# Streaming attention: five 4 MB buffers against 8 MB loads of 64 KB runs into a hand-kept ring of five slots

## The chip, the cores and the metric

The kernel runs on one core of one Trainium2 chip. The metric is the device time in microseconds (us) of one execution; most executions of one kernel agree within 0.3%. PE is the engine for matmuls, DVE the vector engine, ACT the scalar engine, POOL the engine for cross-partition work, SP the engine whose queue issues nearly all loads here. A profile is one execution; its span is some 2 us shorter than the time (1347.8 against 1349.4 us for the kernel before), and spans are compared with spans.

## The reference

One decoding step: attention of 4 queries (one for each batch element) with 32 heads over a K and a V cache of 8192 rows, plus a small gated feed-forward block. Cut to what matters, and partly put in words:

```python
def reference(A_x, A_k_cache, A_v_cache, A_wq, A_wo, B_x, B_w_r, B_w_gate, B_w_up, B_w_down, gate_w):
    # A_x 4x1x1024; k_cache, v_cache 4x32x8192x128; wq 1024x4096; wo 4096x1024; all bf16
    q = (x @ wq) split into 32 heads of 128
    scores = einsum("bhqd,bhkd->bhqk", q, k_cache) * Dh ** -0.5
    a = einsum("bhqk,bhkd->bhqd", softmax(scores), v_cache) -> (4, 1, 4096) @ wo
    b = x + upd     # upd: (silu(x @ w_gate) * (x @ w_up)) @ w_down, times sigmoid(x @ w_r)
    ...             # A_x, B_x and gate_w are combined at the end (cut)
```

K and V together are 537 MB, the weights 39 MB. Each byte is used once, so the kernel is a stream of loads with a little work on each.

## The kernel before

Each load is a 4 MB piece: two heads, each on 64 partitions, 128 rows of 128 numbers in each partition (32 KB per partition). Pieces go into a pool of five buffers. A K piece is transposed on DVE in four steps and multiplied on PE after each step; a V piece takes 32 matmuls with 512 columns. A group of K pieces ends with a softmax, which passes through POOL, DVE and ACT. V follows K by one group.

```python
    ring = ctx.enter_context(tc.tile_pool(name="ring", bufs=5))
    ...
    def slot():
        return ring.tile([P, RING], BF, name="piece", tag="piece")    # RING = 128*128: 32 KB per partition
    ...
    def kv_view(cache, u):
        b, h0 = heads(u)
        return cache[b, h0:h0 + HT].rearrange("h (r j) d -> (h r) (j d)", j=JR)      # HT = 2, JR = 128

    def k_piece(u):
        ...
        kn = slot()
        nc.sync.dma_start(out=kn[:], in_=kv_view(A_k_cache, u))
        for c in range(JR // CJ):                                                    # four steps
            T = ttp.tile([P, CJ, 2, 32, 2], BF, name="T", tag="T")
            nc.vector.transpose(...)                                                 # L336
            ...                                                                      # 8 matmuls into S_ps, L342
        if t == GT - 1:
            softmax(g)
    ...
    for u in range(NT - 2):
        order += [("k", u)] + [("v", u - LAG)] * (u >= LAG)
```

Only PE keeps the written order; on every other engine, and on the SP queue, a scheduler decides the order of instructions when the kernel is built. Each queue is then worked through in that order.

## Time and profile before

Three runs took 1349.28 to 1349.53 us, median 1349.34.

| what | before |
|---|---|
| time, span | 1349.3 us, 1347.8 us |
| bytes of the load queue | 575.68 MB |
| share of the span in which the load queue's packets were under way | 99.5% |
| PE, DVE busy | 79%, 47% |
| a 4 MB load, from issue to landing | 39.4 us |

The page of the profile, its rows of 40 slices (tenths of DMA busy), its queues, its chain of work that ended last, two groups of instructions and the loads of K (count, KB each, median us from issue to landing):

```profile
DMA  9999999999999999999999999999999999999997
DMA packets 22162, 576.22 MB, mean 428 GB/s; under 512 B 2399, under 2 KB 2407, under 8 KB 2925
q1 hardware_dynamic: 22104, 575.68, 99.5%
DMA 50%; PE 30%; DVE 11%; issue 6%; ACT 1%; POOL 1%; SPq 0%; DVEq 0%; ACTq 0%
L336 DVE STREAM_TRANSPOSE T<-piece 128x2048 uint32<-128x2048 uint32 x256 | 576.1, 2288 | 437.0 <-DMA piece<-in_A_k_cache_dram 321.1
L401 PE MATMUL o_ps<-piece,PB 128*16 128x512 bf16 x2048 | 457.6, 382 | 14.8 <-DMA piece<-in_A_v_cache_dram 14.8
piece<-in_A_k_cache_dram SPq DMA_DIRECT2D x64, 4096.0 KB, 39.4
```

(T is the transposed K; S_ps and o_ps are the sums of the K and of the V matmuls.) The stream of loads is the limit: it has no hole, and DVE's largest wait is for K (321.1 us). The chain names PE and DVE for 41% of the span all the same. That is no contradiction: the chain steps from a load to what let it be issued, which is a buffer coming free. As several loads lie queued, that release comes long before the stream needs it. 39.4 us from issue to landing, against 9.7 us that 4 MB take at the full rate, says that about four loads are queued at any time.

The waits of the SP queue before (us in total, times, longest) show the same: SP waits nearly all the time, and it costs nothing.

```profile
SPq L394 <- DVE T L336: 551.3, 57, 21.0
SPq L333 <- PE o_ps L401: 442.1, 52, 10.4
```

### The profile page before, as it was taken

How to read it: one execution, taken by the hardware profiler on the slowest of the kernel's cores; microseconds unless marked ns; L12 is line 12 of the kernel's file. 1: busy time of each engine (PE TensorE's matmuls, PEld its weight loads, DVE VectorE, ACT ScalarE, POOL GpSimd, SP SyncE). 2: the span in 40 equal slices, each digit the busy share in tenths (PEclk: the TensorE clock that was granted, in tenths of full speed). 3: DMA queues.
4: the chain of work that ended last, by engine and by line, in shares of the span. 5: the costliest groups of instructions: out<-in, count | busy, mean ns of one | idle time of the engine just before them, and what ended most of it. 6: DMA issues, size and time to landing. Idle time of an engine off the chain costs nothing.

```text
span 1347.8 us, 8253 instructions
## 1 busy us (share of the span) xinstructions
PE 1059.3 (79%) x4600; PEld 233.2 (17%) x2412; DVE 631.4 (47%) x375; ACT 41.5 (3%) x46; POOL 47.9 (4%) x115
## 2 busy tenths in 40 slices
PE   2667779876978868876998769888788859797878
PEld 0111111211111111111212111211112112121111
DVE  3555755535544554454545454444544456346000
ACT  0000010001000010001000010000000010000000
POOL 2000000000000000000000000000000000000000
PEclk8878989898989989989898879899888979999899
DMA  9999999999999999999999999999999999999997
GB/s 403 433 433 422 433 430 430 432 433 430 430 433 430 430 431 434 429 431 432 433 428 432 433 430 430 433 431 429 432 434 429 428 433 434 429 428 434 432 423 323
DMA packets 22162, 576.22 MB, mean 428 GB/s; under 512 B 2399, under 2 KB 2407, under 8 KB 2925
## 3 DMA queue, kind: packets, MB, share of 16 engines
q1 hardware_dynamic: 22104, 575.68, 99.5%
q8 instruction: 27, 0.44, 0.1%
q14 instruction: 11, 0.08, 0.0%
q10 hardware_dynamic: 20, 0.02, 0.0%
HBM read 575.68 MB, written 0.01 MB: 427 GB/s over the span
## 4 chain that ended last, share of the span: by engine, by line
DMA 50%; PE 30%; DVE 11%; issue 6%; ACT 1%; POOL 1%; SPq 0%; DVEq 0%; ACTq 0%
DMA piece<-in_A_k_cache_dram 40%; PE o_ps L401 16%; PE S_ps L342 13%; DVE T L336 10%; DMA piece<-in_A_v_cache_dram 9%; PE small L419 1%; DMA piece<-in_A_wo_dram 1%; POOL PB L373 1%; DVE PT L367 1%; ACT PTs L365 1%; ACT OS L411 1%; DVE OS L412 1%; POOL tot L377 0%; PE acc L188 0%; PE o_ps L225 0%
## 5 line engine op out<-in xcount | busy, mean ns | idle before, releaser
L336 DVE STREAM_TRANSPOSE T<-piece 128x2048 uint32<-128x2048 uint32 x256 | 576.1, 2288 | 437.0 <-DMA piece<-in_A_k_cache_dram 321.1
L342 PE MATMUL S_ps<-T,Z 128*128 128x512 bf16 x2048 | 544.6, 416 | 246.6 <-DVE T L336 235.3
L401 PE MATMUL o_ps<-piece,PB 128*16 128x512 bf16 x2048 | 457.6, 382 | 14.8 <-DMA piece<-in_A_v_cache_dram 14.8
L342 PEld LDWEIGHTS <-Z 128*128 128x128 bf16 x1024 | 108.0, 105 | 667.2 <-issue 664.3
L401 PEld LDWEIGHTS <-PB 128*16 128x16 bf16 x1024 | 91.9, 90 | 373.1 <-issue 361.3
L412 DVE SCALAR_TENSOR_TENSOR OS<-o_ps,mE,OS 128x512 f32<-128x512 f32 x16 | 12.0, 751 | 174.6 <-ACT OS L411 174.6
L326 POOL TENSOR_TENSOR Z<-qa,mq 128x16 bf16<-128x16 bf16 x64 | 16.7, 262 | 1072.3 <-PE S_ps L342 1054.3
L411 ACT ACTIVATE OS<-o_ps,mE 128x512 f32<-128x512 f32 x16 | 11.0, 687 | 1040.5 <-PE o_ps L401 1040.5
L419 PEld LDWEIGHTS small<-selg,OS 128*128 128x128 f32 x128 | 24.9, 273 | 12.2 <-issue 11.1
L419 PE MATMUL small<-selg,OS 128*128 128x8 f32 x128 | 22.3, 302 | 0.0
L353 DVE TENSOR_REDUCE m<-S_ps 128x1 f32<-128x1024 f32 x8 | 9.8, 1225 | 15.9 <-PE S_ps L342 15.9
L188 PE MATMUL acc<-piece,LT 128*4 128x512 bf16 x64 | 14.9, 378 | 1.7 <-DMA piece<-in_A_wo_dram 1.6
L373 POOL COPY PB<-PT 64x1024 bf16<-64x1024 bf16 x8 | 15.1, 1884 | 29.1 <-DVE rex L375 29.1
L372 ACT COPY PB<-PT 64x1024 bf16<-64x1024 bf16 x8 | 15.3, 1908 | 10.6 <-DVE PT L367 10.6
L367 DVE STREAM_TRANSPOSE PT<-PTs 128x1024 bf16<-128x1024 bf16 x8 | 10.0, 1245 | 11.9 <-ACT PTs L365 11.9
L188 PE MATMUL acc<-piece,hT 128*4 128x512 bf16 x56 | 12.4, 379 | 0.0
L131 PE MATMUL small<-identb,x 6*128 6x6 bf16 x8 | 0.6, 194 | 14.2 <-DVE identb L128 14.2
L379 DVE RECIPROCAL rinv<-tot 128x16 f32<-128x16 f32 x8 | 2.0, 253 | 19.9 <-POOL tot L377 19.9
L365 ACT ACTIVATE PTs<-S_ps,negm 128x1024 bf16<-128x1024 f32 x8 | 8.9, 1113 | 70.0 <-DVE negm L362 70.0
L225 PE MATMUL S_ps<-piece,xw 128*4 128x512 bf16 x64 | 6.6, 591 | 3.0 <-DMA piece<-in_A_wq_dram 3.0
L422 DVE SCALAR_TENSOR_TENSOR OT<-small,sgb,rinv 128x8 bf16<-128x8 f32 x16 | 3.2, 202 | 11.7 <-PE small L419 11.7
L358 POOL PARTITION_ALL_REDUCE gmx<-mex x8 | 3.1, 390 | 81.9 <-issue 50.3
(72 smaller groups left out, 74.6 us busy)
## 6 DMA issues: line engine op xcount, KB each, us to landing
piece<-in_A_k_cache_dram SPq DMA_DIRECT2D x64, 4096.0 KB, 39.4
piece<-in_A_v_cache_dram SPq DMA_DIRECT2D x63, 4096.0 KB, 39.1
piece<-in_A_wq_dram SPq DMA_DIRECT2D x2, 4096.0 KB, 22.1
piece<-in_B_w_gate_dram SPq DMA_DIRECT2D x2, 3584.0 KB, 40.1
piece<-in_B_w_up_dram SPq DMA_DIRECT2D x2, 3584.0 KB, 34.6
piece<-in_A_wo_dram SPq DMA_DIRECT2D x6, 1024.0 KB
piece<-in_B_w_down_dram SPq DMA_DIRECT2D x1, 4096.0 KB, 35.6
piece<-in_A_v_cache_dram SPq DMA_DIRECT2D x4, 1024.0 KB, 32.6
```

Of the source, the lines that this page charges most:

```text
L188: nc.tensor.matmul(out_ap, lhsT=lhsT, rhs=rhs, start=start, stop=True, skip_group_check=True)
L326: nc.gpsimd.tensor_tensor(out=Z[:, :, 31:31 + P].rearrange("p e (s d c) -> p e s d c", s=HT, d=QH)[:, :, :, :, 0], in0=qa[:, :, h0:h0 + HT ...
L336: nc.vector.transpose(out=T[:].rearrange("p j h i e -> p (j h i e)").bitcast(U32), in_=kn[:, c * CJ * Dh:(c + 1) * CJ * Dh].bitcast(U32))
L342: nc.tensor.matmul(sps[:, z, :], lhsT=Z[:, he, s:s + P], rhs=T[:, 16 * z:16 * z + 16, half, :, e], start=(t == 0 and c == 0 and he == 0), ...
L365: nc.scalar.activation(out=PTs[:], in_=sps[:].rearrange("p z n -> p (z n)"), func=ACT.Exp, bias=negm[:, 0:1], scale=scale, accum_out=rs[:, ...
L367: nc.vector.transpose(out=PT[:].rearrange("p j i -> p (j i)"), in_=PTs[:])
L372: nc.scalar.copy(out=Bv[0:W, :, :, 0, :], in_=Pv[0:W])
L373: nc.gpsimd.tensor_copy(out=Bv[W:P, :, :, 1, :], in_=Pv[W:P])
L401: nc.tensor.matmul(o_ps[row:row + NM, e, :], lhsT=B_[:, JT * t + c, z, w].rearrange("p e s j -> p (e s j)"), rhs=vn[:, j0 * Dh:(j0 + 4) * ...
L411: nc.scalar.activation(out=o_sb[:], in_=o_ps[:, 0, :], func=ACT.Copy, scale=mE[:, 0:1])
L412: nc.vector.scalar_tensor_tensor(out=o_sb[:], in0=o_ps[:, 1, :], scalar=mE[:, 1:2], in1=o_sb[:], op0=ALU.mult, op1=ALU.add)
L419: nc.tensor.matmul(oT[:, :], lhsT=o_sb[:, q * Dh:(q + 1) * Dh], rhs=selg[:, q].rearrange("p t s -> p (t s)"), start=(q == 0), stop=(q == 3))
```

## The change

Its intent: half as many packets, each twice as long. A load now brings 8 MB: four heads, each on a quadrant of 32 partitions, 64 KB in one run from the cache to each partition. It fills two neighbouring slots of a ring of five, kept by hand as one tile. The pairs take slots (0,1), (2,3), (4,0), (1,2), (3,4), and again; one pair in five wraps, and its destination is written with a step of −4 slots. The weights are loaded the same way, except wo and the last V pair, which come in smaller pieces. A K pair has eight transposes, a V pair 64 matmuls of twice as many output rows; the total work on DVE and PE is the same. A group of the softmax is now four pairs of four heads (it was eight pieces of two heads).

```diff
-    ring = ctx.enter_context(tc.tile_pool(name="ring", bufs=5))
+    NS = 5
+    ring = const.tile([P, NS, RING], BF, name="ring")
+    turn = [0]
+
+    def slots(n):
+        at = turn[0]
+        turn[0] = (at + n) % NS
+        return at
+
+    def load_pair(src, n):
+        a = slots(2)
+        step = 1 if a + 1 < NS else 1 - NS
+        dst = ring[:, a:a + 2, 0:n] if step == 1 else ring[:, NS - 1::1 - NS, 0:n]
+        ins = nc.sync.dma_start(out=dst, in_=src.rearrange("p (s n) -> p s n", s=2))
+        if n < RING:
+            WIDE[ins.ins.name] = 2 * n          # weights: the read is rewritten as one run (cut)
+        return [ring[:, a], ring[:, (a + 1) % NS]]
-        return cache[b, h0:h0 + HT].rearrange("h (r j) d -> (h r) (j d)", j=JR)
+        return cache[b, h0:h0 + NQ].rearrange("h (r j) d -> (h r) (j d)", j=2 * JR)
-        kn = slot()
-        nc.sync.dma_start(out=kn[:], in_=kv_view(A_k_cache, u))
-        for c in range(JR // CJ):
+        ks = load_pair(kv_view(A_k_cache, d), RING)
+        for n in range(RD):
+            kn, c = ks[n // JT], n % JT
-        vn = slot()
+            vs = load_pair(vv, RING)
     ... (masks, weights and softmax copies for four heads instead of two are cut)
```

## The prediction

> **What bounds the kernel now.** The DMA stream. The page's 40 slices show DMA at 9 tenths throughout and 422 to 434 GB/s; windows of 50 us show a DMA share of 1.00 and 426 to 433 GB/s. 575.7 MB at 431.5 GB/s is 1334 of the span's 1347.8 us; the rest is start and tail. PE is busy 79%, DVE 47%, and neither sets the pace: the largest DVE wait is for K transfers (321 us). The 4 MB transfers take 39 us from issue to landing, four times the 9.7 us that each needs: four lie queued, so the queue hides slow releases.
>
> **What the change brings.** Twice as long reads halve the packets (22,104 now). The Trainium skill (DMA: Bandwidth & Descriptors, "Where 436 GB/s comes from") puts the fabric's ceiling at 435 GB/s; the trace's 431.5 leaves at most 0.8%, 11 us. I expect about half: 5 us. Compute is the same: 256 transposes of 2.27 us, 2048 + 2048 matmuls of 512 columns.
>
> **What it costs.** Five slots hold two and a half 8 MB transfers of 19.4 us. Transfer n+1 needs slots of n-1 freed while n flies; that alone would fit: half a K pair is four transposes (8.9 us), half a V pair 32 matmuls (7.07 us), both under 19.4. But the built program's waits are wider for the transfers that wrap (slots 4 and 0, two in ten). They wait for the last transpose of the newest K pair, in slots they don't touch. And the scheduler then puts the next K load ahead of a wrapped V or weight load on the in-order SP queue. The same page says (Anatomy of one DMA) that waits are done on the issuing sequencer, so everything behind waits too. Walking the built order with the trace's durations (estimates; about 3 us from issue to landing beyond the transfer, as the first K piece shows: 12.6 MB issued from 0.8 us are there at 33.1):
> - Seven times (K1, K4, K9, K14, K19, K24, K29) a K load waits for half of the K pair just landed, with nothing in flight: 8.9 to 10 us of transposes + 3 = 12 to 13 us idle; 90 in all, and 10 more where the softmax of a group end delays DVE.
> - Seven times (up, V0, V5, V10, V15, V20, V25) the load after a wrapped one waits for that one to land and for half of its matmuls: 7 to 8.7 us + 3 = 10 to 12; 77 in all.
> - Six wrapped K loads wait for all eight transposes of the K pair before (18 us against a flight of 19.4): 2.6 each, 16 in all.
>
> DMA is the critical path, so all of it shows: 1349 + 193 - 5, less some 12 for a shorter start-up latency than I took: **1525 us**, range 1490 to 1560. Faster by 2%: 0.02; within 2%: 0.05; slower: 0.93.
>
> **What would show it.** Slices of the page with DMA at 4 to 7 tenths, about every 200 us, and 429 to 435 GB/s between; packets near 12,000; mean some 380 GB/s. In the SP queue's waits: loads waiting for transposes and o_ps matmuls in the order above, K1 before the gate's weights. In the chain: the K transfers' share down, transposes and o_ps up. Landing of K about 20 to 35 us for 8 MB. PEclk lower around the holes.
>
> **What would make it wrong.** If both sides of the wait are shorter than I think (idle restart under 3 us, PE warm), 1490. If 64 KB reads are slower per byte, later still. If the wide waits do not hold SP in the order built, the stream stays full and the time is about 1343 us.

## More of the kernel before

The third, fourth and fifth run are read for large differences only.

## The result, and the profile after

Four runs of the changed kernel took 1564.91 to 1566.71 us, median 1565.66, beside 1349.42 us for the kernel before on the same chip. The ratio is 1.1603, with a 95% interval of 1.1586 to 1.1619: 16% slower. (Ratios here are the mean time of one kernel's fast runs over that of the other's of the same rounds, so not quite the ratio of the medians.)

The same lines of the page after; the last but one is from the trace's full list of loads, and has no size as it takes in the K pairs of more than one form:

```profile
DMA  9689769995978996889996798996798976799997
DMA packets 13279, 576.20 MB, mean 368 GB/s; under 512 B 1326, under 2 KB 1334, under 8 KB 1852
q1 hardware_dynamic: 13224, 575.68, 86.2%
DMA 52%; PE 23%; issue 14%; DVE 10%; POOL 1%; ACT 1%; DVEq 0%; SPq 0%; ACTq 0%
L356 DVE STREAM_TRANSPOSE T<-ring 128x2048 uint32<-128x2048 uint32 x256 | 570.2, 2281 | 663.3 <-DMA ring<-in_A_k_cache_dram 370.3
L428 PE MATMUL o_ps<-ring,PB 128*32 128x512 bf16 x2048 | 463.6, 388 | 164.7 <-DMA ring<-in_A_v_cache_dram 164.7
ring<-in_A_k_cache_dram SPq DMA_DIRECT2D x26, 28.7
ring<-in_A_k_cache_dram SPq DMA_DIRECT2D x6, 8192.0 KB, 22.7
```

The work per instruction is unchanged: 256 transposes at 2281 ns instead of 2288, 2048 V matmuls at 388 ns instead of 382. What changed is the first row: the stream has holes, and the load queue is under way for 86.2% of a longer span. Multiplied by the spans, the shares give a simple ledger: 0.862 × 1565.0 = 1349 us of transfer instead of 0.995 × 1347.8 = 1341, so 8 us more; and 216 us idle instead of 7, so 209 us more. (The shares are rounded; the packet times themselves add up to 1348.3 and 1340.9 us, so 7.4 us more.) The spans differ by 217 us. Six K loads, the wrapped ones, now land 22.7 us after they were issued (the median); 8 MB alone take 19.4 us, so nothing was in front of them: they were issued into an empty queue.

The waits of the SP queue after:

```profile
SPq L128 <- DVE T L356: 536.4, 45, 21.0
SPq L128 <- DMA ring<-in_A_k_cache_dram: 408.6, 24, 41.0
SPq L128 <- DMA ring<-in_A_v_cache_dram: 216.0, 12, 32.8
SPq L128 <- PE o_ps L428: 211.9, 24, 10.8
```

The total of waits on transposes is hardly changed (it was 551 us). What is new are the long waits for landings, 408.6 and 216.0 us, where the K and V loads of the kernel before waited 23.7 us for landings of K and 10.7 for those of V. But not even these show that the stream is empty: the first split kernel below waits 188.0 and 145.8 us for them in its unsplit loads alone, and has hardly a hole. What matters is whether anything is in flight while SP waits. Windows of 50 us show that (columns: stretch, length, busy us of PE, its weight loads, DVE, ACT and POOL, the PE clock, DMA share, GB/s). The first line is the kernel before, the fence after it the changed kernel:

```profile
350.00:400.00 50.00, 40.74 (x170) 8.17 (x85) 20.62 (x11) 0.69 (x1) 0.79 (x3) 0.93 1.00 431
```

```profile
350.00:400.00 50.00, 36.10 (x158) 8.64 (x82) 27.23 (x20) 5.70 (x5) 4.85 (x5) 0.90 0.60 253
400.00:450.00 50.00, 18.76 (x75) 3.79 (x36) 7.17 (x4) 0.00 (x0) 0.26 (x1) 0.69 0.79 336
450.00:500.00 50.00, 40.08 (x168) 8.43 (x84) 24.10 (x11) 0.00 (x0) 0.26 (x1) 0.93 1.01 438
```

Two holes stand in the first two stretches, of 19.3 and 11.5 us, and the third is full. The semaphore waits in the built program, with the slots named, say why. Loads are in the order in which the SP queue holds them; K8 is K pair 8, counted from 0, and V4 V pair 4:

```text
changed kernel, as built                          waits for
K8  -> slots 2,3
K9  -> slots 1,2      4th transpose of K8         (slot 2 is K8's first half)
V4  -> slots 4,0      8th transpose of K8         (K8 is in 2,3: none of V4's slots)
V5  -> slots 3,4      landing of V4, half of V4's matmuls
```

K9 was written after V4, and is placed ahead of it. It takes the slot of K8's first half, so it cannot be issued before K8 has landed and been half transposed, and nothing else is in flight then. V4 and V5 stand behind it. The profile's chain through this hole (start us, us, what; in order of time) ends with K8's transposes and the wait for V4:

```profile
359.88 13.93 PE o_ps L428 x64
373.83 0.69 ACT OS L438
374.55 0.75 DVE OS L439
375.31 0.09 DVE gmm L380
...
378.30 0.06 POOL PB L396
378.36 1.86 issue
380.21 1.89 POOL PB L396
382.20 0.46 POOL tot L400
382.68 0.04 DVE rinv L402
382.85 2.27 DVE T L356
...
402.69 32.44 DMA ring<-in_A_v_cache_dram
```

The first engine of the 16 runs dry at 375.2 us and the last is at work again at 395.9. K9 is issued at 393.9, V4 at 402.7, V5 at 444.8 (42 us after V4, as SP has to wait until V4 has landed and 32 of its matmuls are done). The pattern comes back seven times, once in every five pairs.

### The profile page after: what moved, and what is told of

Read it like the earlier page. It is cut to its first block, busy times and chain, and to the rows that moved or that the text cites. A ratio compares the mean times of both kernels' runs of the same rounds, so it can differ in the third digit from the quotient of the medians.

```text
span 1565.0 us, 7946 instructions
## 1 busy us (share of the span) xinstructions
PE 1047.8 (67%) x4536; PEld 227.7 (15%) x2348; DVE 621.9 (40%) x358; ACT 51.1 (3%) x46; POOL 57.1 (4%) x91
## 2 busy tenths in 40 slices
DMA packets 13279, 576.20 MB, mean 368 GB/s; under 512 B 1326, under 2 KB 1334, under 8 KB 1852
## 3 DMA queue, kind: packets, MB, share of 16 engines
q1 hardware_dynamic: 13224, 575.68, 86.2%
## 4 chain that ended last, share of the span: by engine, by line
DMA 52%; PE 23%; issue 14%; DVE 10%; POOL 1%; ACT 1%; DVEq 0%; SPq 0%; ACTq 0%
DMA ring<-in_A_k_cache_dram 34%; DMA ring<-in_A_v_cache_dram 14%; PE o_ps L428 11%; DVE T L356 9%; PE S_ps L362 9%; DMA ring<-in_B_w_down_dram 2%; DMA ring<-in_B_w_gate_dram 2%; PE acc L209 2%; POOL PB L396 1%; PE small L445 1%; PE o_ps L243 0%; DVE PT L387 0%; ACT PTs L385 0%; DVE OS L439 0%; ACT OS L438 0%
## 5 line engine op out<-in xcount | busy, mean ns | idle before, releaser
L356 DVE STREAM_TRANSPOSE T<-ring 128x2048 uint32<-128x2048 uint32 x256 | 570.2, 2281 | 663.3 <-DMA ring<-in_A_k_cache_dram 370.3
L362 PE MATMUL S_ps<-T,Z 128*128 128x512 bf16 x2048 | 529.3, 406 | 262.6 <-DVE T L356 262.4
L428 PE MATMUL o_ps<-ring,PB 128*32 128x512 bf16 x2048 | 463.6, 388 | 164.7 <-DMA ring<-in_A_v_cache_dram 164.7
L428 PEld LDWEIGHTS <-PB 128*32 128x32 bf16 x1024 | 100.9, 99 | 523.6 <-issue 487.9
L209 PE MATMUL acc<-ring,hT 128*4 128x512 bf16 x56 | 15.2, 441 | 29.5 <-DMA ring<-in_B_w_down_dram 29.5
L396 POOL COPY PB<-PT 32x1024 bf16<-32x1024 bf16 x16 | 30.1, 1880 | 45.1 <-DVE rex L398 44.7
L394 ACT COPY PB<-PT 32x1024 bf16<-32x1024 bf16 x16 | 30.5, 1906 | 9.4 <-DVE PT L387 9.3
L209 PE MATMUL acc<-ring,LT 128*4 128x512 bf16 x64 | 14.5, 379 | 0.7 <-DVE LT L308 0.7
L445 PEld LDWEIGHTS small<-selg,OS 128*128 128x128 f32 x64 | 10.8, 242 | 7.3 <-issue 4.8
L445 PE MATMUL small<-selg,OS 128*128 128x16 f32 x64 | 9.9, 289 | 0.9 <-DVE OS L439 0.9
## 6 DMA issues: line engine op xcount, KB each, us to landing
ring<-in_A_k_cache_dram SPq DMA_DIRECT2D x6, 8192.0 KB, 22.7
```

The lines of the kernel that those rows point to most:

```text
L209: nc.tensor.matmul(out_ap, lhsT=lhsT, rhs=rhs, start=start, stop=True, skip_group_check=True)
L356: nc.vector.transpose(out=T[:].rearrange("p j h i e -> p (j h i e)").bitcast(U32), in_=kn[:, c * CJ * Dh:(c + 1) * CJ * Dh].bitcast(U32))
L362: nc.tensor.matmul(sps[:, z, :], lhsT=Z[:, he, s:s + P], rhs=T[:, 16 * z:16 * z + 16, half, :, e], start=(t == 0 and n == 0 and he == 0), ...
L394: nc.scalar.copy(out=Bv[at, :, :, q, :], in_=Pv[at])
L396: nc.gpsimd.tensor_copy(out=Bv[at, :, :, q, :], in_=Pv[at])
L428: nc.tensor.matmul(o_ps[row:row + NM, e, :], lhsT=B_[:, RD * t + c, z, w].rearrange("p e s j -> p (e s j)"), rhs=vn[:, j0 * Dh:(j0 + 4) * ...
```

## The experiments

The theory: two things together empty the queue. First, waits wider than needed: a wrapped load waits for the newest K pair in slots that it does not touch. Second, the order: the scheduler puts a K load that depends on the pair just landed ahead of a load that could go. Rivals: (1) 64 KB runs or 8 MB transfers are slow by themselves; (2) two and a half pairs in the ring are too shallow, whatever the waits; (3) the work per pair is slower; (4) the order on the SP queue alone is the cause.

### Splitting the transfers

In the first run only the wrapped pairs are sent as two transfers of 4 MB, one for each slot; everything else is the changed kernel.

```diff
-        step = 1 if a + 1 < NS else 1 - NS
-        dst = ring[:, a:a + 2, 0:n] if step == 1 else ring[:, NS - 1::1 - NS, 0:n]
-        ins = nc.sync.dma_start(out=dst, in_=src.rearrange("p (s n) -> p s n", s=2))
+        halves = src.rearrange("p (s n) -> p s n", s=2)
+        if a + 1 == NS:
+            for i, at in enumerate((a, 0)):
+                nc.sync.dma_start(out=ring[:, at, 0:n], in_=halves[:, i])
+            return [ring[:, a], ring[:, 0]]
+        ins = nc.sync.dma_start(out=ring[:, a:a + 2, 0:n], in_=halves)
```

> The changed kernel, but each wrapped pair (slots 4 and 0) is loaded as two 4 MB transfers, so that its waits are only for the two slots it fills; the other four fifths stay 8 MB transfers of 64 KB runs. Theory (the wide waits of the wrapped loads, and the queue order that follows from them, drain the DMA queue): the holes go, 1344 to 1356 us, DMA queue busy over 97% of the span. Rival 1 (8 MB transfers of 64 KB runs are slower in themselves, or land later): stays above 1540. Rival 2 (a ring of two and a half transfers is too shallow, whatever the waits): 1420 to 1560.

Measured: 1357.97 us (1356.39 to 1359.49, five runs), ratio 1.006. It misses the range by 2 us and takes back 208 of the 216 us. In the built program the waits are exact, and the order is the written one. The SP queue of this run at the same place (V4's two halves, then K9):

```profile
308.43 9.29 SPq L129 DMA_DIRECT2D ring<-in_A_v_cache_dram  x2
346.60 0.33 SPq L131 DMA_DIRECT2D ring<-in_A_k_cache_dram  x1
```

In the second run every pair is sent as two transfers (the same edit without the condition), so that 64 KB runs no longer exist either.

> The changed kernel, with every pair loaded as two 4 MB transfers of 32 KB runs (64 KB apart in memory): layout, masks and matmuls stay those of the change. Theory: no holes and no longer runs, so within 0.3% of the kernel before, 1346 to 1353 us, and some 3 us over the run with only the wrapped pairs split, since in the changed kernel's trace a 64 KB packet that doesn't start a hole took 2428 ns against 2 x 1217 before (0.3%). Rival 3 (the head-per-quadrant layout or its wider matmuls cost the time): near 1565.

Measured: 1350.52 us (1349.07 to 1350.86, five runs), ratio 1.0006 (0.9993 to 1.0018): the kernel before, within noise. The time is in the range, but the expected order of the two is wrong: this one is 7 us below the first, not 3 above. The load queues of the two pages, first the wrapped pairs split, then all:

```profile
q1 hardware_dynamic: 13688, 575.68, 98.6%
```

```profile
q1 hardware_dynamic: 21464, 575.68, 99.4%
```

0.986 × 1357.8 = 1339 us of transfer with mostly 64 KB packets, 0.994 × 1349.0 = 1341 with 32 KB. The long reads are worth some 2 us in 1341 here, and the first split kernel loses more than that in four holes of 1 to 2.4 us (at 344, 658, 972 and 1130 us). They are taken up below. Rivals 1 and 3 fall: the layout with a head per quadrant, the 64 KB runs, the larger softmax group and the ring by hand all run at the speed of the kernel before, once the transfers are split.

### The order alone, and the wide waits alone

The third run is the changed kernel with the SP queue kept in written order: `manual_schedule(engines={PE, SP})` instead of `{PE}`. The wide waits stay.

> The changed kernel with the loads issued in the order in which they are written (no K load ahead of a wrapped V or weight load), the wide waits kept. Theory: seven holes remain, each longer (all eight transposes of the K pair in front of the wrapped load, 18 us + 3, in place of four) and the seven holes behind wrapped loads go: 1530 to 1560 us. Rival 4 (the reordering in the queue alone is the cause): 1350 to 1400.

Measured, one look: 1557.37 us. It is in the range; rival 4 falls. The slices of its page:

```profile
DMA  9499499996599995998994997993999974998997
```

The holes are fewer and deeper. Before K9's place the stream is now idle for 30.9 us instead of 19.3, as V4 waits there for all eight transposes of K8; the holes behind the wrapped loads are gone.

The fifth run has exact waits (wrapped pairs split as in the first run) and the changed kernel's order: the SP queue is kept in written order, and the K load is written ahead of the wrapped load, as the scheduler had put it.

```diff
+    early = {}
-    def load_pair(src, n):
+    def load_pair(src, n, kd=None):
         ...
         if a + 1 == NS:
+            if kd is not None:
+                early[kd] = load_pair(kv_view(A_k_cache, kd), RING)
-        ks = load_pair(kv_view(A_k_cache, d), RING)
+        ks = early.pop(d) if d in early else load_pair(kv_view(A_k_cache, d), RING)
-            vs = load_pair(vv, RING)
+            vs = load_pair(vv, RING, d + LAG + 1 if d + LAG + 1 < ND else None)
     ... (the same for the gate and down weights)
```

> The run with only the wrapped pairs split (exact waits, 1358 us), with one thing put back: on the SP queue each wrapped V or weight load again stands behind the K load that follows it. Theory: the order by itself makes the seven holes in which a K load waits for half of the K pair just landed, 12 to 20 us each, and none of the others, as the first half of the pair behind lands 9.7 us before the second: 1440 to 1480 us. Rival (only the wide waits drain the queue, the order is a symptom): 1355 to 1375.

Measured, one look: 1470.77 us, in the range. Its seven K holes (103 us in all) are nearly as in the changed kernel (108); the holes behind the wrapped loads shrink to 1.3 to 2.2 us each. Its SP queue, with K9 and then V4's two halves:

```profile
371.92 0.33 SPq L134 DMA_DIRECT2D ring<-in_A_k_cache_dram  x1
372.30 0.90 SPq L132 DMA_DIRECT2D ring<-in_A_v_cache_dram  x2
```

It also shows what the order does on its own: V4, which needs the same slots as in the first run, is issued at 372.3 us, right after K9 at 371.9; in the first run its halves went at 308.4 and 317.4 us, 38 and 29 us ahead of K9. The four kernels make a table (us):

| | written order | K load ahead |
|---|---|---|
| exact waits | 1358 | 1471 |
| wide waits | 1557 | 1566 |

The causes do not add up: each alone empties the queue (113 and 199 us), and both together cost 208. With wide waits the order hardly matters. The wide waits are the heavier cause, and they were also what led the scheduler to the other order: where only the transfers were split, it kept the written one.

One rival was not run by itself: the split also makes the wrapped loads finer, and not only their waits exact. The first run's trace speaks against it at V4. The second half, too, was issued at 317.4 us, 10 us before K8 landed (327.5), so one load of 8 MB with the waits of both halves would, by this estimate, still have come in time.

### One slot less

The fourth run has `NS = 4` and nothing else changed. No pair wraps then.

> The changed kernel with four slots in place of five: a ring of just two 8 MB transfers, so no transfer wraps and all waits are exact, with less memory in all. Theory: no long hole is left, but each K load waits for all of the V pair or K pair two before it, a hole of 2 to 5 us for each of 32: 1430 to 1490 us, faster than the changed kernel with one slot less. Rival 2 (too shallow a ring is the cause): slower than 1565.

Measured, one look: 1475.23 us, in the range and 90 us faster than with five slots. Rival 2, as the cause of the 216 us, falls: less space is faster where it takes the wrap away. Depth does cost something: the page shows a busy share of 92.1%, and the trace some thirty holes of 1.5 to 7 us, as each 8 MB load waits in the built program for the whole of the pair before the last one, as expected.

```profile
DMA  9889998999898989999899998999899988999997
```

### The long holes at two group ends

The prediction came out 41 us low, so the sizes needed a look too. Of the seven holes before K loads, five are 11.9 to 14.6 us long, but those before K9 and K29 are 19.3 and 22.4. Both follow the first K pair of a group (K8, K28), whose transposes begin late: the chain above shows the scaling of the last group's output (OS) between the softmax's steps on DVE, with 64 V matmuls ahead of it, and then the reciprocal of the sums (rinv), which waits for two copies on POOL; only then comes the first transpose.

Two runs kept the written order on DVE as well (`engines={PE, DVE}`), which puts the OS step behind the softmax: the sixth in the kernel with split wraps, the seventh in the changed kernel.

> The run with only the wrapped pairs split, with DVE too in the order in which the program is written, so that the softmax of a K group is not held up behind the scaling of o_ps, which waits for 64 matmuls of V. Theory (the four holes of about 2 us that are left in that run at 345, 660, 973 and 1131 us come from K transposes that start some 5 us late for this): the holes go and the 0.2% of longer runs shows: 1345 to 1352 us. If the holes have another cause: 1356 to 1360.

> The changed kernel with DVE in the order in which the program is written, nothing else. Theory (the part of the miss that I put down to the softmax at a group's end: the holes before K9 and K29 are 19.3 and 22.4 us of mean idle where those before K14, K19 and K24 are 12.6 to 14.6): those two shrink by 5 to 8 us each, 1548 to 1558 us. If their length has another cause: 1563 to 1567.

Measured: 1372.00 us (1366.65 to 1372.95, four runs) instead of 1358, and 1578.17 us (1576.69 to 1580.25, four runs) instead of 1566. Both expectations failed: both kernels got slower. The timeline of the seventh run around K8's transposes shows why (start us, us, engine, line, operation, and in brackets the idle time before with what ended it):

```profile
376.35 1.25 DVE L387 STREAM_TRANSPOSE PT<-PTs 128x1024 bf16<-128x1024 bf16 x1 [4.74 <-ACT PTs L385]
382.11 0.25 DVE L402 RECIPROCAL rinv<-tot 128x16 f32<-128x16 f32 x1 [4.40 <-POOL tot L400]
382.85 2.30 DVE L356 STREAM_TRANSPOSE T<-ring 128x2048 uint32<-128x2048 uint32 x1
390.43 0.25 DVE L448 SCALAR_TENSOR_TENSOR OT<-small,sgb,rinv 128x16 bf16<-128x16 f32 x1 [5.28 <-PE small L445]
```

The wait was moved, not taken away: the exponential waits 4.7 us on ACT, where the first OS step still stands ahead of it; the reciprocal still waits for POOL; and the step that makes OT now stands ahead of the second transpose and waits 5.3 us for PE. This says nothing against the cause, only that the edit did not remove it.

The ninth run removes it properly, in the changed kernel: written order on PE, DVE and ACT, the OT step behind the fourth transpose, and the reciprocal moved into that step.

```diff
-    ctx.enter_context(tc.manual_schedule(engines={PE}))
+    ctx.enter_context(tc.manual_schedule(engines={PE, DVE, ACT}))
-            if n == 0:
+            if n == 3:
                 flush()
-        rinv = stat.tile([P, GH], F32, tag="rinv")
-        nc.vector.reciprocal(out=rinv[:], in_=tot[:])
-        rinv_t[g] = rinv
+        rinv_t[g] = tot
         def finish():
             ...
+            rinv = stat.tile([P, GH], F32, tag="rinv")
+            nc.vector.reciprocal(out=rinv[:], in_=rinv_t[g][:])
```

> The changed kernel with the written order kept on PE, DVE and ACT, the OT step moved behind the fourth transpose of its K pair, and the reciprocal of the sums moved to that step, so that neither the scaling of OS nor the wait for the sums stands before the first transposes of a group's next K pair. The order on the SP queue is as in the changed kernel. Theory: the holes before K9 and K29 are 6 and 9 us longer than the other K holes because DVE begins K8's and K28's transposes late, behind those steps. Expected: these two holes 13 to 16 us instead of 19.3 and 22.4, and 1551 to 1560 us. Rival: the length of these holes comes from elsewhere (the softmax itself, or where the K8 load stands): both holes stay over 18 us and the time 1562 to 1570 us.

Measured: 1554.09 us (1553.02 to 1555.40, four runs), in the range, 11.6 us faster than the changed kernel. The order of its SP queue in the built program was compared with the changed kernel's and is the same. The hole before K29 is 13.9 us instead of 22.4, as expected; the one before K9 is 16.4 instead of 19.3, a little over the range. Its DVE timeline at the same place:

```profile
374.38 0.19 DVE L398 TENSOR_SCALAR rex<-mask,rs 128x16 f32<-128x16 f32 x1
379.11 0.75 DVE L437 SCALAR_TENSOR_TENSOR OS<-o_ps,mE,OS 128x512 f32<-128x512 f32 x1 [4.54 <-ACT OS L436]
379.78 4.49 DVE L356 STREAM_TRANSPOSE T<-ring 128x2048 uint32<-128x2048 uint32 x2
385.84 4.50 DVE L356 STREAM_TRANSPOSE T<-ring 128x2048 uint32<-128x2048 uint32 x2 [1.56 <-PE S_ps L362]
```

K8's transposes begin at 379.8 us instead of 382.9 (K8 itself landed 0.8 us earlier, so the gain is 2.3 us), and what holds them now is the OS step again, 4.5 us behind ACT. So the cause is confirmed: it is DVE's in-order queue at the group end. Not all of its delay is gone, which fits the 3 us that the hole before K9 still has over the others. One other hole, at 949 us, grew by 4 us, and the other holes and the tail changed by up to 2.2 us each, some 6 us less in all. So it is the two holes that carry the evidence (11.3 us together); that the total agrees with them so well is in part luck.

### Versions that might beat both

The eighth run goes back to split transfers. It was made in the belief that the first run's four small holes come from K loads that wait for the second of slots 1 and 2. It splits those pairs as well (`if a in (1, NS - 1)`), and keeps 64 KB runs for the other three in five.

> The kernel of the first run (wrapped pairs sent as two 4 MB transfers, the other pairs as one of 8 MB), with the pairs of slots 1 and 2 sent as two as well, so that the first half goes as soon as slot 1 is free. Theory: the 8 us that the first run keeps over the kernel before are its four small holes, which stand before K loads that wait for the second of their two slots. Expected: 1346 to 1352 us, at most one hole of over 1 us in the stream. Rival: the holes come from K loads standing late in the queue's order, and splitting moves only the wait: 1355 to 1359 us.

Measured: 1355.42 us (1352.28 to 1356.76, five runs), ratio 1.0047 (1.0034 to 1.0061). It misses the theory's range and falls just inside the rival's. The belief was also wrong on its face: in the built program the four holes stand before K9, K17, K25 and K29, and only K9 and K29 go to slots 1 and 2. What the four share is that each is the second K pair of a softmax group. The profiled execution, the fastest of the five, still has a hole of 1.4 us before K25; the others, 2 to 4 us longer, have no trace.

That points to the group ends again. The last two runs take the kernels of the first and the eighth run and add the ninth run's edits; their SP queues keep the order they had.

> The kernel of the first run (wrapped pairs split, 1358 us) with the ninth run's edits for the group ends; the order on the SP queue is the same. Its four small holes (8 us in all) stand before K9, K17, K25 and K29, each the second K pair of a softmax group, into slots 1 and 2, 3 and 4, 0 and 1, and 1 and 2. Theory: they come from the late first transposes of a group, as the long holes of the changed kernel did, and not from the slots: holes gone or under 1 us each, 1347 to 1353 us. Rival: they come from 8 MB loads that wait for their second slot, whatever DVE does: 1355 to 1360 us.

> The kernel of the eighth run (wrapped pairs and pairs of slots 1 and 2 split, 1355 us) with the ninth run's edits for the group ends; the order on the SP queue is the same. Theory: with both the stream has no hole, and 64 KB runs in three pairs of five save some 1 to 2 us of transfer: 1346 to 1350 us, equal to the kernel before within 0.3%. If the time lost in the eighth run's untraced executions came from something else than holes at group ends, 1353 to 1357 us.

Measured: 1351.45 us (1349.98 to 1352.05, five runs), ratio 1.0014 (1.0001 to 1.0026), and 1351.89 us (1350.71 to 1352.40, five runs), ratio 1.0018 (1.0004 to 1.0032). The tenth is in its range, and 6.5 us faster than the first: in its trace the four holes are gone, and nothing between start and tail is longer than a microsecond. The theory of the late group ends holds there too. The eleventh misses its range by 2 us: splitting slots 1 and 2 as well brings nothing further. The load queue of the tenth run's page:

```profile
q1 hardware_dynamic: 13688, 575.68, 99.1%
```

0.991 × 1349.7 = 1338 us of transfer, 3 us less than before the change, and the tail is 3.4 us longer (10.8 us idle in place of 7.5), so that the two nearly even out. So the changed layout, with exact waits and an undisturbed group end, is level with the kernel before. No version is faster than it; a stream that is 99.5% full leaves little.

## Why the prediction was right or wrong

The direction and the mechanism were right, and shown: the stream is the limit; the wide waits and the order on the SP queue empty it seven times; the classes of holes stand where the prediction put them; splitting the wrapped transfers alone takes nearly all of it back. The reading that the Trainium skill's page supported (DMA: Bandwidth & Descriptors, "Anatomy of one DMA": waits are done on the issuing sequencer) agrees with these traces: in the fifth run V4, whose slots had long been free, went out 0.4 us after K9 that stood in front of it. (The section is written about the path of the GPSIMD queue; here SP issues.)

The size was not: 1566 us lies just above the range of 1490 to 1560. The sum's terms, with what the trace shows for each (idle time as the mean over the 16 DMA engines):

| term of the prediction | predicted, us | measured, us |
|---|---|---|
| seven K loads behind half of the K pair just landed | 90 + 10 | 108.4 |
| seven loads behind a wrapped one | 77 | 75.7 |
| six wrapped K loads behind eight transposes | 16 | 20.5 |
| longer reads (measured: all of the transfer time) | −5 | +7.4 |
| "less some 12 for a shorter start-up latency than I took" | −12 | not there |
| start and tail | 0 | +3.4 |
| sum | 176 | 215 of 216 |

The agreement of the second row is in part luck: the hole before the up weights is 6.1 us and not 10, and the other six are 10.7 to 12.5.

The steps that failed:

- **"less some 12 for a shorter start-up latency than I took".** This took back part of a loss that had just been worked out, on a guess. An ordinary hole shows that 3 us was if anything too little: K13's transposes begin at 610.2 us, K14 is issued at 619.1 after 8.9 us of them, and the stream is idle for 12.6 us, so stopping and starting cost 3.7 us. The term was 12 us of the 41.
- **"1349 + 193 - 5".** The longer reads do save: a 64 KB packet in a full stream takes 2428 ns, two of 32 KB 2435 (0.3%), and the first split kernel needs 2 us less transfer time than the kernel before. But a packet of 64 KB that begins after a hole takes 3021 ns on average (243 of them in the trace), some 0.6 us more, and with twenty holes the transfer time grew by 7.4 us. The term was off by 12 us. It was read as a property of the transfers, when it depends on whether the stream runs.
- **"10 more where the softmax of a group end delays DVE".** The mechanism was right, and the ninth run shows it; the two holes exceed the other five's mean of 13.3 us by 6.0 and 9.1, so 15 us. Together with the five others, at 13.3 us instead of 12 to 13, this class was 8 us short.
- The six wrapped K loads cost 3.4 us each instead of 2.6 (4.5 in all), and the tail grew by 3.4 us, which the prediction had left out.

Most of the prediction's other marks held: slices of 5 to 8 tenths, full rate between the holes, a mean of 368 GB/s where some 380 was said, 13,279 packets where near 12,000 was said (the wrapped pairs' packets of 32 KB make the difference; with four slots, where nothing wraps, there are 11,816). One mark failed: in the chain the K transfers' share fell, from 40% to 34%, but the transposes and the o_ps matmuls did not rise (10% and 16% before, 9% and 11% after); V transfers (9% to 14%) and "issue" (6% to 14%) did. (The window from 450 us reads 438 GB/s with a DMA share of 1.01; a share over one says that a little too much is booked to it, so the rates of whole runs are the ones to compare.) "If 64 KB reads are slower per byte, later still" was not needed: they are not slower in a full stream. The Trainium skill's ceiling of 435 GB/s (the same page, "Where 436 GB/s comes from") agrees: no kernel here held more over its whole run than the 428 GB/s of the kernel before, and the room above that proved worth 1 to 4 us of transfer time in the split kernels with long reads.

## What to carry to other kernels

When a stream is already 99% full, look first at how many loads are in flight, and only then at the size of one. A transfer of twice the size into the same space halves the number of loads that can wait in the queue, and a load that reaches over two slots waits for the later of them. Read the waits and the order in the built program whenever a destination is strided or wraps around; here wider waits than needed, for one pair in five, cost 199 us with the loads in written order, and a changed order alone cost 113. In a sum of losses, do not subtract a guess from a loss that was read from the trace.

## What the Trainium skill lacked or had wrong

- DMA: Bandwidth & Descriptors, "Rules for kernel authors" and "Measured (HBM→SBUF, 128 partitions, SWDGE, issued from GpSimd)", give a lower bound for the size of a transfer (1 MiB and more) and an efficiency that still rises at 16 MB (97%). They have no word on the other side: with a fixed space, larger transfers leave fewer in flight. Here 8 MB in place of 4 MB saved 1 to 4 us of transfer time in 1341 where the stream ran; a ring of just two such loads, with exact waits, took 1475 us (one look) where five buffers of 4 MB take 1349.
- The same page, "Anatomy of one DMA — SWDGE (gpsimd) path", fits a fixed cost of about 2.0 us for a DMA on that path. For the loads of this kernel, which SP issues, the eight K and V loads that were issued into an idle stream, and whose landing the trace tells, took 21.8 to 23.6 us from issue to landing, 2.4 to 4.2 us over their 19.4 us of transfer, and a hole in the stream (the one before K14) cost 3.7 us over the work that it waited for. What a stopped stream costs to restart, as one figure, is on no page that I found.
- The same page, "Where 436 GB/s comes from", says that for transfers between HBM and SBUF the HBM side (about 358 GB/s) binds. With one core at work the kernel before held 428 GB/s over its whole span and 426 to 433 in full windows of 50 us. The page's section on measured bandwidth gives that figure for two cores at work, and 425 GB/s for one alone; the sentence itself lacks the condition.
- GPSIMD Engine Reference, section 4.1, recommends this engine for reductions across partitions, and section 3.2 gives one time, for a large tile. No page that I found has a time for a small one: the all-reduce of the maxima, a tile of 128x16, shows 0.39 us busy here (times on POOL are rough), but DVE waited 10.25 us for it at a group end in the ninth run. It is not the price of every such call: in the changed kernel that of the sums, right behind two copies on POOL, ended with them in a wait of 4.4 us, of which the copies took 3.8. Why the first one waits is open.
